# A list schedule made three times: due times of loads that know the kernel's own transposes, a third x buffer and another spacing of score units

## The chip, the cores and the metric

The kernel runs on one core of a Trainium2 chip. The metric is the time of one execution on the device in microseconds (us), less being better; every version is timed over several runs, and one further execution of each is taken with the hardware profiler. The core's engines are TensorE (PE, the matmuls; its weight loads are listed as PEld), VectorE (DVE), ScalarE (ACT), GpSimd (POOL) and SyncE (SP). Each works through its own instructions in program order, and they wait for each other by semaphores. Transfers run on the core's DMA engines; here SP, POOL and once ACT issue them.

## What is computed

Attention over a sliding window of 128 tokens with 4 sink tokens that all may see, 4 batches of 8 heads, 768 tokens, 64 elements a head; then, on the 3072 tokens of 512 elements, a gated feed-forward with two products more. There is no softmax beyond the attention's, so that the last two matrices can be folded into one.

```
scores = q @ k.T / sqrt(64)
keep   = (key < 4) | (0 <= query - key < 128)
x      = softmax(where(keep, scores, -1e9)) @ v        # heads side by side: 3072 x 512
h      = ((x @ w1) * (x @ w2)) @ w3                    # 1024 wide
out    = h @ w_out                                     # 3072 x 512, float32
```

## The kernel before

All matmuls are in bfloat16. w3 and w_out are multiplied once at the start: w3 is transposed on PE (`fold_w3`, L402 to 414) and multiplied with w_out (`fold_mm`, L427), so that each token tile needs one projection. Five of the eight row blocks of w3 and all of w_out come as float32 through SP ("raws", L142, L162) and are cast by ACT and DVE (L418); the other w3 rows, w1, w2, and all of q, k and v come through POOL, which casts on the way (L104 to 139), in the order of the list `order` (L146).

The attention goes batch by batch (b), tile by tile of 256 tokens (t = 0 to 2), head pair by head pair (r = 0 to 3). A unit of scores (`scores`, L255, and `block_scores`, L274, for the first two tiles of batch 0) is: the score matmuls into one of two large PSUM buffers, the exponential on ACT, the mask on DVE. Then `values` (L335, L299) multiplies with v on PE, and DVE divides by the row's sum and writes the result into a buffer xn (L357, L320), one for each tile of 256 tokens. Keys and queries must stand transposed: for batches 0 and 1 PE does it (L211, copied by DVE at L213), a block of 128 tokens at a time; for batches 2 and 3 (`XPOSE`) the DMA does it, issued by SP (`transposes_dma`, L216), two DMAs for each block of 128 tokens. The same holds for x: batches 0 and 1 on PE (L330, L367), batches 2 and 3 by a DMA from SP (`x_transposes_dma`, L375), two for each tile.

The feed-forward of a batch goes over chunks of 384 tokens (256 in batch 0). A gate task (`gate`, L384) makes 128 of the 1024 columns for a chunk: four matmuls with w1, which ACT copies to SBUF, and four with w2, which DVE multiplies with that copy. A first gate of a 384-token chunk reads xT of one tile and a half. A projection (`project`, L448) is eight matmuls for 128 tokens, a copy by ACT and a store by SP.

What stands when on each engine is settled while the program is built. Every piece of work is a task with a priority, a list of stages (engine and cost in us), the tasks it follows, the loads it needs and its kind of PSUM buffer (`task`, L519 and on). The loop from L732 on is a list scheduler: it keeps a clock for each engine, takes for PE the task that can begin soonest and, of those that can begin at once, the one of the lowest priority number, and emits its instructions. A score unit may begin only PACE us after the one before (L660, L698; the index is the tile, or for batch 0's block units their number). The gates and projections have high priority numbers; they fill what is left. When a load is due is worked out beforehand by `landings` (L481): two queues, SP's raw loads and POOL's, each load with a service time, a lag and a share of the DMA engines. SP's queue is one of the scheduler's engines (costs of 1.3 and 1.4 for a transpose, `XP_US` 8.0 and `XX_US` 6.0 until it has landed, L517, L567, L628). POOL's loads are not scheduled; they are emitted in `order`. Where PE would be idle early on, `keep_busy` (L462) puts matmuls on zeros in.

Since the engines work in program order, the schedule sets only the order; the times on the chip follow from it and from what the waits find.

Of the kernel before, what the change touches and what calls it, by code (L numbers as in the profile page):

```python
# [21 lines left out]
def kernel(  # L22
# [276 lines left out]
    def block_values(b, j, r0):  # L299

        t, i = j // 2, j % 2
        av = ps_mm.tile([P, 2, 2, D + 1], FP32, tag="mm", name="av")
        todo = []
        for r in range(r0, r0 + 2):
            if t > 0:
                q0 = (t - 1) * 256 + i * P
                todo.append((av[:, r - r0, :, :].rearrange("p e d -> p (e d)"), es[b][:, q0:q0 + P],
                             vs[b][:, 2 * r:2 * r + 2, :].rearrange("p e d -> p (e d)")))
            am, kbs = ams.pop((b, j, r))
            for s, kb in enumerate(kbs):  # L310
                for e in range(2):
                    todo.append((av[:, r - r0, e, :], am[:, e, s, :], vN[b][:, kb, 2 * r + e, 0:D + 1]))
        for n, (o, lhs, rhs) in enumerate(todo):
            nc.tensor.matmul(o, lhs, rhs, start=(n == 0), stop=(n == len(todo) - 1),  # L314
                             skip_group_check=True)
        yield
        rec = work.tile([P, 2, 2, 1], FP32, tag="rec", name="rec")
        nc.vector.reciprocal(rec[:], av[:, :, :, D:D + 1])
        if i == 0 and r0 == 0:
            xns[b, t] = work.tile([P, 2, NP, 2, D], BF16, tag="xn", bufs=2, name="xn")  # L320
        nc.vector.tensor_mul(xns[b, t][:, i, r0:r0 + 2, :, :], av[:, :, :, 0:D],
                             rec[:].to_broadcast([P, 2, 2, D]))
        yield
# [11 lines left out]
    def values(b, r, t):  # L335
# [20 lines left out]
        if r == 0:  # L356
            xns[b, t] = work.tile([P, 2, NP, 2, D], BF16, tag="xn", bufs=2, name="xn")  # L357
# [123 lines left out]
    def landings(RAW=2.0, POOL=3.0, DGE=1.3, RAMP=(0.33, 0.64, 0.66, 0.9)):  # L481

        queues = {"sp": [(RAW, 1.31, 1.0, [("raw",) + x[:3]]) for x in raws],
                  "pool": [(gen, us, 2.2, keys) for x in order for gen, us, keys in service(*x)]}
# [3 lines left out]
        while any(at[n] < len(q) for n, q in queues.items()):  # L488
            while len(ready) < len(queues["pool"]) and (len(ready) < 8 or len(landed) > len(ready) - 8) \
# [6 lines left out]
                ready.append(max(5.8, issue + DGE))  # L496
            busy = [n for n, q in queues.items() if at[n] < len(q)
# [15 lines left out]
    landings()  # L513

    tasks = {}
    SP_US = 0.7
    XP_US, XX_US = 8.0, 6.0  # L517
# [40 lines left out]
    for b in range(B):  # L558
        for t in range(NT):
# [66 lines left out]
            if b in X_XPOSE:  # L626
                for i in range(2):
                    task(("xd", b, t, i), 1, x_transposes_dma(b, t, i), [("sp", 1.3), ("dma", XX_US)],  # L628
                         [("av", b, NP - 1, t)])
# [30 lines left out]
    PACE = [0.0, 3.4, 3.5, 5.5]  # L660
    TURN, SHAPE = 0.095, {"sc": 1, "ss": 2}
    last_sc, shape = 0.0, 0
    START, WARM_UNTIL = 1.2, 40.0
    BACKLOG = 1.6
    free = {"pe": 0.0, "act": 0.0, "dve": 0.0, "sp": 0.0}
    rings = {n: [[0.0] for _ in range(k)] for n, k in (("mm", 4), ("sc", 2))}
    done, begun = {}, set()
    queue = {"act": [], "dve": [], "sp": []}

    def spare(ring):  # L670
        return sorted((c for c in rings[ring] if c[0] is not None), key=lambda c: c[0])

    def occupy(ring, cell):
        old = spare(ring)[0]
        rings[ring] = [c for c in rings[ring] if c is not old] + [cell]

    def pe_pick():
        best = None
        for k in tasks.values():
            kind = k["name"][0]  # L680
            if k["name"] in begun or any(a not in begun for a in k["started"]) \
                    or k["stages"][0][0] != "pe":
                continue
            if any(a not in (begun if k["half"] else done) for a in k["after"]):
                continue
            est = max([free["pe"]] + [arrive[x] + HOP for x in k["loads"]])
            if not k["half"]:
                est = max([est] + [done[a] + HOP for a in k["after"]])
            if k["ring"]:
                slots = spare(k["ring"])[:k["slots"]]  # L690
                if len(slots) < k["slots"]:
                    continue
                est = max([est] + [c[0] + HOP for c in slots])
            if est > free["pe"]:
                est += MARGIN.get(kind, 0.0)
            if k["paced"]:
                busy = max(0.0, free["act"] - free["pe"]) + sum(q[2] for q in queue["act"])
                est = max(est, free["pe"] + busy - BACKLOG, last_sc + (PACE[k["name"][1]]))  # L698
            wait = est - free["pe"]
            key = (0.0 if wait < 0.05 else wait, k["prio"])  # L700
            if best is None or key < best[0]:
                best = (key, k, est)
        return best

    def when(q):

        at, _, _, k = q
        if k["half"]:
            return max(at, done[k["after"][0]] + HOP) if k["after"][0] in done else None
        return at  # L710

    def advance(k, at):

        i = k["stage"]
        if k["ring"] and i == 1:
            k["cell"][0] = at
        if i == 1 and "frees" in k:
            tasks[k["frees"]]["cell"][0] = at
        k["stage"] = i + 1
        if i + 1 < len(k["stages"]):  # L720
            e, us = k["stages"][i + 1]
            if e == "dma":
                k["stage"] += 1
                done[k["name"]] = at + us
                return
            queue[e].append((at + HOP, YIELD.get(k["name"][0], 0.1), us, k))
        else:
            done[k["name"]] = at

    later = [x for x in order if x[0] == "qkv" and x[1] > 0]  # L730
    folds = [x for x in tasks if x[0] in ("c", "t3", "fm")]
    while len(done) < len(tasks):  # L732
        if later and all(x in done for x in folds):
            for x in later:
                load(*x)
            later = []
        for k in tasks.values():
            e, us = k["stages"][0]
            if e != "pe" and k["name"] not in begun and all(a in done for a in k["after"]):
                begun.add(k["name"])  # L740
                k["stage"] = 0
                at = max([arrive[x] for x in k["loads"]] + [done[a] for a in k["after"]])
                queue[e].append((at + HOP, YIELD.get(k["name"][0], 0.0), us, k))
        pe = pe_pick()
        moves = [(pe[2], 0, "pe")] if pe else []
        picks = {}
        for e in ("act", "dve", "sp"):
            ready = [(max(free[e], when(q)) + q[1], when(q), n)
                     for n, q in enumerate(queue[e]) if when(q) is not None]
            if ready:  # L750
                picks[e] = queue[e][min(ready)[2]]
                moves.append((max(free[e], when(picks[e])), 1, e))
        start, _, e = min(moves)
        if e == "pe":
            k = pe[1]
            gap = start - max(free["pe"], START)
            if gap > 0.5 and start < WARM_UNTIL and spare("mm") \
                    and spare("mm")[0][0] <= max(free["pe"], START):
                keep_busy(int((gap - 0.25) / (0.22 if start > 9.0 else 0.43)))
                occupy("mm", [max(free["pe"], START)])  # L760
            begun.add(k["name"])
            k["stage"] = 0
            us = k["stages"][0][1]
            if SHAPE.get(k["name"][0], 0) != shape:
                shape = SHAPE.get(k["name"][0], 0)
                us += TURN
            if k["paced"]:
                last_sc = start
            if k["ring"]:
                k["cell"] = [None]  # L770
                occupy(k["ring"], k["cell"])
        else:
            q = picks[e]
            queue[e].remove(q)
            us, k = q[2], q[3]
        next(k["gen"])
        free[e] = start + us
        advance(k, free[e])
# [34 lines left out]
```

## Time and profile before

| | |
|---|---|
| median of 3 runs | 198.18 us |
| their range | 197.58 to 199.52 us |
| the profiled execution, its own time | 197.96 us |
| its span, first to last instruction | 196.3 us |
| mean granted clock of TensorE | 0.998 |
| DMA packets, bytes | 104165, 28.35 MB |
| the same, mean over the span | 144 GB/s |

The page gives the busy time of each engine and the chain of work that ended last. The chain in order of time lists its pieces with start, length and name; a piece with x8 is eight instructions of one kind. The timeline lists an engine's instructions, with idle time before them in brackets and what ended it. The DMA view gives packets, bytes and the time from issue to landing; narrowed to one issue, its line is about that one transfer. Lines such as L452 are those of the kernel above. In a row of the windows stand the stretch, the busy time of each engine with its number of instructions, the granted clock, the share of the DMA engines and GB/s.

### The profile page before, as it was taken

What the parts mean: (1) busy time and instruction counts of PE and PEld (TensorE: products, weight loads), DVE (VectorE), ACT (ScalarE), POOL (GpSimd) and SP (SyncE); (2) the same over time, 40 slices, a digit from 0 to 9 for tenths busy, and PEclk for the clock granted to TensorE, in tenths of its full rate; (3) what the DMA queues carried; (4) which work ended last, traced back from release to release, by engine and by line L of the source; (5) the groups of instructions that cost most, each with busy time, mean ns of one, the idle gap of its engine ahead of it and who ended that gap; (6) DMA issues with size and microseconds to landing.
All of it is one profiled execution on the core that took longest, in us unless ns stands there. A gap on an engine that the chain in (4) does not pass through costs nothing.

```text
span 196.3 us, 4494 instructions
## 1 busy us (share of the span) xinstructions
PE 188.9 (96%) x1781; PEld 118.8 (61%) x1795; DVE 114.6 (58%) x268; ACT 105.2 (54%) x174; POOL 75.4 (38%) x104
## 2 busy tenths in 40 slices
PE   7799999999999999999999999999999999999994
PEld 2345566898856687666666655666555566654443
DVE  4455787764876878687879738777644034440000
ACT  4242557845726788886777255556653333332332
POOL 5199878579999853555364300000000000000000
PEclk9999999999999999999999999999999999999999
DMA  6999999999999999999999999930222600002334
GB/s 225 395 365 154 182 163 197 194 158 154 155 155 210 186 172 123 154 168 175 127 130 157 119 155 129 168 79 2 53 110 107 183 33 3 0 0 98 142 141 157
DMA packets 104165, 28.35 MB, mean 144 GB/s; under 512 B 95184, under 2 KB 99664, under 8 KB 104144
## 3 DMA queue, kind: packets, MB, share of 16 engines
q0 software_dynamic: 79520, 12.33, 91.8%
q1 hardware_dynamic: 24480, 15.67, 36.6%
q8 instruction: 14, 0.23, 0.5%
q14 instruction: 7, 0.06, 0.1%
q10 hardware_dynamic: 144, 0.07, 0.1%
HBM read 29.36 MB, written 6.29 MB: 182 GB/s over the span
## 4 chain that ended last, share of the span: by engine, by line
PE 86%; DMA 7%; DVE 3%; issue 1%; ACT 1%; SPq 1%; POOL 0%
PE pg L391 41%; PE po L452 19%; PE av L351 6%; PE sc L261 5%; DMA qN<-in_q_dram 4%; PE pw L438 3%; DMA ab<-in_moe_w_dram 3%; PE ph L438 3%; PE tp L211 2%; PE tp L408 1%; PE av L314 1%; PE xt L367 1%; PE sc L282 1%; DVE w3t L413 1%; PE sp L243 1%
## 5 line engine op out<-in xcount | busy, mean ns | idle before, releaser
L391 PE MATMUL pg<-xT,w_sb 128*128 128x384 bf16 (+1 forms) x576 | 91.0, 308 | 0.0
L391 PEld LDWEIGHTS <-w_sb 128*128 128x128 bf16 x576 | 53.6, 98 | 25.4 <-issue 0.5
L395 DVE TENSOR_TENSOR ab<-a_sb,pg 128x384 bf16<-128x384 f32 (+1 forms) x72 | 36.6, 508 | 29.0 <-PE pg L391 24.9
L398 ACT COPY a_sb<-pg 128x384 f32<-128x384 f32 (+1 forms) x72 | 31.9, 444 | 36.1 <-DVE ab L395 17.7
L452 PE MATMUL po<-w3o,ab 128*128 128x512 bf16 (+2 forms) x198 | 42.6, 362 | 0.5
L266 ACT ACTIVATE ex<-sc 128x1024 bf16<-128x1024 f32 (+1 forms) x40 | 37.8, 964 | 5.4 <-PE sc L261 4.8
L452 PEld LDWEIGHTS <-ab 128*128 128x128 bf16 x208 | 19.3, 98 | 20.1 <-issue 0.3
L456 ACT COPY w_sb<-po 128x512 f32<-128x512 f32 (+2 forms) x25 | 14.1, 565 | 26.0 <-PE po L452 24.1
L270 DVE TENSOR_TENSOR am<-ex,maskt 128x1024 bf16<-128x1024 bf16 (+1 forms) x40 | 25.4, 645 | 3.8 <-ACT ex L266 3.8
L108 POOL DMA_DIRECT2D vN<-in_v_dram x24 | 21.5, 894 | 12.1 <-DMA kN<-in_k_dram 11.2
L108 POOL DMA_DIRECT2D qN<-in_q_dram x24 | 21.7, 904 | 7.9 <-DMA vN<-in_v_dram 5.8
L108 POOL DMA_DIRECT2D kN<-in_k_dram x24 | 21.8, 908 | 7.3 <-DMA qN<-in_q_dram 4.2
L358 DVE TENSOR_TENSOR xn<-av,rec 128x256 bf16<-128x256 f32 x40 | 17.0, 424 | 1.4
L351 PE MATMUL av<-vN,am 128*128 128x65 bf16 x296 | 16.4, 193 | 0.0
L351 PEld LDWEIGHTS <-am 128*128 128x128 bf16 x296 | 14.3, 97 | 2.5 <-issue 0.2
L355 DVE RECIPROCAL rec<-av 128x4 f32<-128x4 f32 x40 | 7.2, 179 | 11.5 <-PE av L351 11.3
L261 PE MATMUL sc<-kqT 64*128 64x128 bf16 (+1 forms) x216 | 11.6, 238 | 0.0
L351 PE MATMUL av<-vs,es 128*128 128x130 bf16 x56 | 11.0, 221 | 0.1
L213 DVE COPY kqT<-tp 128x1024 bf16<-128x1024 bf16 x12 | 8.3, 691 | 4.4 <-PE tp L211 4.3
L438 PE MATMUL ph<-wo_sb,w3t 128*128 128x512 bf16 x32 | 8.6, 380 | 1.4 <-ACT wo_sb L418 0.9
L456 DVE COPY w_sb<-po 128x128 f32<-128x128 f32 x1 | 0.3, 292 | 16.3 <-ACT w_sb L456 16.3
L261 PEld LDWEIGHTS <-kqT 64*128 64x128 bf16 x216 | 6.9, 94 | 4.0 <-issue 3.2
(71 smaller groups left out, 143.9 us busy)
## 6 DMA issues: line engine op xcount, KB each, us to landing
out_dram<-w_sb SPq DMA_DIRECT2D x23, 256.0 KB, 2.2
kN<-in_k_dram POOLq DMA_DIRECT2D x24, 128.0 KB, 8.2
qN<-in_q_dram POOLq DMA_DIRECT2D x24, 128.0 KB, 8.0
vN<-in_v_dram POOLq DMA_DIRECT2D x24, 128.0 KB, 7.8
w_sb<-in_moe_w_dram POOLq DMA_DIRECT2D x9, 256.0 KB, 8.9
ab<-in_moe_w_out_dram SPq DMA_DIRECT2D x3, 512.0 KB, 5.8
ab<-in_moe_w_dram SPq DMA_DIRECT2D x3, 512.0 KB, 6.6
kN<-in_moe_w_out_dram SPq DMA_DIRECT2D x1, 512.0 KB, 8.9
```

What stands on the lines that cost most here:

```text
L108: nc.gpsimd.dma_start(out=dst, in_=rows(src, b, kb))
L261: nc.tensor.matmul(sc[:, e, c:c + n], kT[b][hp, r, kb * P:(kb + 1) * P], qT[b][hp, r, qb * P:qb * P + n], start=True, stop=True)
L266: nc.scalar.activation(ex[:, :, c0:], sc[:, :, c0:], ACTF.Exp, scale=scale)
L270: nc.vector.tensor_mul(am[:, :, c0:], ex[:, :, c0:], mk)
L351: nc.tensor.matmul(o, lhs, rhs, start=(n == 0), stop=(n == len(todo) - 1), skip_group_check=True)
L358: nc.vector.tensor_mul(xns[b, t][:, :, r, :, :], av[:, :, :, 0:D], rec[:].to_broadcast([P, 2, 2, D]))
L391: nc.tensor.matmul(pg[:], w_sb[:, kk, dt * P:(dt + 1) * P], xT[b][:, kk, tk], start=(kk == 0), stop=(kk == NP - 1))
L395: nc.vector.tensor_mul(ab[b][:, dt, tk], gate_a.pop((b, c, dt))[:], pg[:])
L398: nc.scalar.copy(a_sb[:], pg[:])
L438: nc.tensor.matmul(po, w3T[i][:, j, :], wo_sb[:, j, :], start=(j == 0), stop=(j == KFF - 1))
L452: nc.tensor.matmul(po[:], ab[b][:, kk, m * P:(m + 1) * P], w3o[:, kk, n0:n1], start=(kk == 0), stop=(kk == KFF - 1))
L456: (nc.vector.tensor_copy if n0 == DM // 2 else nc.scalar.copy)(o_sb, po[:])
```

## The change

The scheduler becomes a function `plan(emit)`, and it runs three times. The first two runs emit nothing; they return at which times SP would issue its DMAs (`taken`), and the next call of `landings` holds up all loads by 1.2 us for each transpose and by 0.6 us for each store, from 4 us after its issue on. The third run emits the program. Before, the loads of q and k of batches 2 and 3 had a flat 1.2 us more of service time instead.

The constants of `landings` change too (service time, lag and ramp in the diff). A DMA transpose counts as landed 8.4 us after its issue, 5.0 us late in the loads and 2.7 us after the last of them, for 8.0 and 6.0 before. PACE goes from 3.4, 3.5, 5.5 to 4, 4.5, 4.5. The buffers xn are three for two. No computing instruction is added or removed but for the matmuls on zeros, of which four go; the order of the tasks changes on PE, ACT, DVE and SP. POOL's instructions keep their order, and one of its loads (the last block of k of batch 1) waits for PE too.

On SP, the stores and transposes stand in another order. Of the transposes in batches 2 and 3, before had (k, q: blocks of 128 tokens of batch 3; x: tiles of 256 tokens of batch 2)

```
k0  x0 x0  q0 k1 q1  x1 x1  k2 q2 k3 q3  x2 x2  (store)  k4 q4 k5 q5
```

and the changed kernel has

```
k0 q0 k1 q1 k2 q2  x0 x0  k3 q3 k4  x1 x1  q4 k5  (store)  q5  (store)  x2 x2
```

The core of the diff, the indentation of the loop's body left out:

```diff
-            xns[b, t] = work.tile([P, 2, NP, 2, D], BF16, tag="xn", bufs=2, name="xn")
+            xns[b, t] = work.tile([P, 2, NP, 2, D], BF16, tag="xn", bufs=3, name="xn")
...
-            return [(0.95 if i[0] == 0 else 0.87, 0.845 + (1.2 if i[0] in XPOSE and x != "v" else 0.7 if (x, *i) == ("v", 0, 4, 5) else 0.0), [(x, i[0], kb)])
+            return [(0.95 if i[0] == 0 else 0.87, 0.845, [(x, i[0], kb)])
...
-    def landings(RAW=2.0, POOL=3.0, DGE=1.3, RAMP=(0.33, 0.64, 0.66, 0.9)):
+    def landings(taken, RAW=2.0, POOL=3.0, DGE=1.3, RAMP=(0.6, 0.95, 0.85, 0.9)):
-        queues = {"sp": [(RAW, 1.31, 1.0, [("raw",) + x[:3]]) for x in raws],
-                  "pool": [(gen, us, 2.2, keys) for x in order for gen, us, keys in service(*x)]}
+        queues = {"sp": [(RAW, 1.28, 1.0, [("raw",) + x[:3]]) for x in raws],
+                  "pool": [(gen, us, 1.8, keys) for x in order for gen, us, keys in service(*x)]}
+        taken, owed = sorted((t + 4.0, us) for t, us in taken), 0.0
...
+            while taken and taken[0][0] <= now:
+                owed += taken.pop(0)[1]
+            if owed > 0.0:
+                owed -= 0.02
+                now += 0.02
+                continue
...
-    landings()
-    XP_US, XX_US = 8.0, 6.0
...
-                        task(qk[-1], 1, transposes_dma(src, dst, kb), [("sp", 1.4), ("dma", XP_US)],
+                        task(qk[-1], 1, transposes_dma(src, dst, kb), [("sp", 1.4), ("dma", 1.2)],
...
-    PACE = [0.0, 3.4, 3.5, 5.5]
+    PACE = [0.0, 4, 4.5, 4.5]
...
+    def plan(emit):
...
-                done[k["name"]] = at + us
+                    end = max(arrive.values())
+                    done[k["name"]] = at + (8.4 if at < end - 4.0 else 5.0 if at < end else 2.7)
...
+            if e == "sp":
+                taken.append((start, 1.2 if k["name"][0] != "p" else 0.6))
+            if emit:
+                next(k["gen"])
...
+    taken = []
+    for last in (False, False, True):
+        landings(taken)
+        taken = plan(last)
```

More of the change, by code (lines that the diff above doesn't have):

```diff
@@ L356, in values @@
         if r == 0:
-            xns[b, t] = work.tile([P, 2, NP, 2, D], BF16, tag="xn", bufs=2, name="xn")
+            xns[b, t] = work.tile([P, 2, NP, 2, D], BF16, tag="xn", bufs=3, name="xn")
         nc.vector.tensor_mul(xns[b, t][:, :, r, :, :], av[:, :, :, 0:D],
@@ L627 @@
                 for i in range(2):
-                    task(("xd", b, t, i), 1, x_transposes_dma(b, t, i), [("sp", 1.3), ("dma", XX_US)],
+                    task(("xd", b, t, i), 1, x_transposes_dma(b, t, i), [("sp", 1.3), ("dma", 1.2)],
                          [("av", b, NP - 1, t)])
@@ L659 @@
     YIELD = {"g": 0.0, "av": 0.0, "sc": 0.4, "tdk": 1.5, "tdq": 1.5}
-    PACE = [0.0, 3.4, 3.5, 5.5]
+    PACE = [0.0, 4, 4.5, 4.5]
     TURN, SHAPE = 0.095, {"sc": 1, "ss": 2}
-    last_sc, shape = 0.0, 0
     START, WARM_UNTIL = 1.2, 40.0
     BACKLOG = 1.6
[L665 to L691, printed above, removed]
-                    continue
[L693 to L723, printed above, removed]
-                done[k["name"]] = at + us
[L725 to L728, printed above, removed]
@@ L740 @@
                 begun.add(k["name"])
                 k["stage"] = 0
[L742 to L775, printed above, removed]
@@ L776 @@
-        next(k["gen"])
-        free[e] = start + us
-        advance(k, free[e])
+                us = k["stages"][0][1]
+                if SHAPE.get(k["name"][0], 0) != shape:
+                    shape = SHAPE.get(k["name"][0], 0)
+                    us += TURN
+                if k["paced"]:
+                    last_sc = start
+                if k["ring"]:
+                    k["cell"] = [None]
+                    occupy(k["ring"], k["cell"])
+            else:
+                q = picks[e]
+                queue[e].remove(q)
+                us, k = q[2], q[3]
@@ L781 @@
+            if e == "sp":
+                taken.append((start, 1.2 if k["name"][0] != "p" else 0.6))
+            if emit:
+                next(k["gen"])
+            free[e] = start + us
+            advance(k, free[e])
+        return taken
+    taken = []
+    for last in (False, False, True):
+        landings(taken)
+        taken = plan(last)
 _INS = ['q', 'k', 'v', 'n_sink', 'window', 'moe_w1', 'moe_w2', 'moe_w3', 'moe_w_out']
```

97 lines of the change are left out of this document (87 added, 10 removed).

## The prediction

> **What bounds the kernel now.** I read the page first, then the waits, then the chain in order of time.
>
> ```profile
> span 196.3 us, 4494 instructions
> PE 188.9 (96%) x1781; PEld 118.8 (61%) x1795; DVE 114.6 (58%) x268; ACT 105.2 (54%) x174; POOL 75.4 (38%) x104
> PE 86%; DMA 7%; DVE 3%; issue 1%; ACT 1%; SPq 1%; POOL 0%
> ```
>
> TensorE (PE) is busy for 96% of the span. A busy share can hide stretched work, so the waits come next.
>
> ```profile
> PE pz L466 <- DVE ksbd L171: 1.3, 1, 1.3
> PE ph L438 <- ACT wo_sb L418: 0.9, 1, 0.9
> PE pw L438 <- DVE w3t L413: 0.4, 1, 0.4
> PE tp L211 <- DMA qN<-in_q_dram: 0.4, 1, 0.4
> PE ph L438 <- DVE w3t L413: 0.3, 1, 0.3
> ```
>
> 3.3 us in all, 1.3 of it ahead of the first instruction. A new order can win very little and can lose much. What PE's work costs shows in the chain (start, us, what):
>
> ```profile
> 20.20 0.33 PE sc L282 x8
> 22.38 0.45 PE tp L211 x8
> 24.37 0.55 PE sc L282 x16
> 33.56 1.75 PE pg L391 x16
> 60.13 0.44 PE sc L261 x8
> 143.15 1.73 PE po L452 x8
> 149.34 0.71 PE av L351 x20
> 155.23 20.80 PE pg L391 x128
> 187.09 6.26 PE po L452 x44
> ```
>
> Start to start, a gate matmul takes 0.163 us (384 columns) or 0.109 (256), a projection of eight matmuls 1.73, a score matmul 0.028 (eight more cost 0.22). So of the 0.33 us of eight score matmuls 0.11 is the turn to their 64-row shape. PE ends at 187.09 + 6.26 = 193.35. Between the last wait for raw weights (13.74, below) and that end, the pitches times the counts of the program's order fill 177.9 of 179.6 us: gates 62.5 + 20.9, projections 41.6, folds 10.8, av 14.4 (0.36 for ten), scores 9.6, transposes 10.2 (0.056 each), the small rest 1.8, 57 turns 6.0. Only 1.7 us after 13.74 is waiting.
>
> **The change part by part.**
>
> *PE's work.* The changed order holds the same matmuls, but 15 warm-up matmuls for 19, and 59 turns of shape for 57: +0.2 us. The warm-up ones cost nothing, for they fill waits:
>
> ```profile
> 1.33 4.83 PE L466 MATMUL pz<-ksbd 128*128 128x512 bf16 x15 [1.33 <-DVE ksbd L171]
> 8.63 0.59 PE L438 MATMUL ph<-wo_sb,w3t 128*128 128x512 bf16 x2 [0.92 <-ACT wo_sb L418]
> 13.12 2.08 PE L438 MATMUL ph<-wo_sb,w3t 128*128 128x512 bf16 x8 [0.30 <-DVE w3t L413]
> 12.64 1.04 ACT L418 CAST wo_sb<-kN 128x1024 bf16<-128x1024 f32 x1 [1.51 <-DMA kN<-in_moe_w_out_dram]
> ```
>
> The second pair of the row at 13.12 needs the last wo rows, whose cast ACT ends at 12.64 + 1.04: it starts at 13.74. Up to there both orders run through the same raw loads and casts in turn, so that the new due times for these (about 1 us earlier) win nothing. From 13.74 on, the changed order without any wait would end at 193.35 - 1.7 + 0.2 = 191.9. That is the floor, 1.5 us under before.
>
> *Loads of batches 0 and 1.* Before let PE reach each tile late. The changed plan believes in landings about 2 us earlier, and its order goes up to the edge. The last tile is the one that counts: the q half of the last PE transposes.
>
> ```profile
> 62.68 0.39 PE L211 MATMUL tp<-ident,qN 128*128 128x128 bf16 x4
> ```
>
> ```profile
> 55.00 0.92 POOL L108 DMA_DIRECT2D qN<-in_q_dram  x1
> ```
>
> ```profile
> qN<-in_q_dram POOLq DMA_DIRECT2D x1, 128.0 KB, 6.9
> ```
>
> That load (the DMA view narrowed to the one issue) lands at 61.9. Ahead of this point the changed order has one projection less (-1.73), four x transposes more (+0.22) and two turns more (+0.21): 1.30 us less work. Before reached it at 62.68 after 1.6 us of waits, so without waits the changed order is there at 62.68 - 1.62 - 1.30 = 59.76, and it must wait 2.2 us, in small pieces at the loads before it or at once. POOL issues these loads in the same order (its one new wait, on PE at batch 1's last k, is for folded w3 that PE is done with some 25 us before) and the DMA engines are full (155 GB/s, below), so they won't land earlier. The rest is then 193.35 - 62.68 + 1.73 - 0.22 = 132.2, and the end 61.95 + 132.2 = 194.1: +0.8 us. The DVE wait of before (0.4) and this load's neighbour (0.4) fall away; this takes their place.
>
> *SP's queue and batch 3.* SP issues in program order: the DMA transposes of k and q (L218), those of x (L378), the stores.
>
> ```profile
> 93.49 1.19 SPq L218 DMA_TRANSPOSE kqT<-kN  x1
> 94.77 3.91 SPq L378 DMA_TRANSPOSE xT<-xn  x2
> 98.78 2.44 SPq L218 DMA_TRANSPOSE kqT<-qN  x1
> 104.42 3.15 SPq L378 DMA_TRANSPOSE xT<-xn  x2
> 107.67 2.42 SPq L218 DMA_TRANSPOSE kqT<-kN  x1
> 118.87 1.23 SPq L218 DMA_TRANSPOSE kqT<-kN  x1
> ```
>
> Before, the x transposes of batch 2's tiles 0 and 1 go out at 94.77 and 104.42, ahead of k block 2 (107.67) and k block 4 (118.87) of batch 3. The changed queue has tile 0 behind q block 2, and tile 1 behind k block 4, as that k is due at 107.7 by the new plan's own `landings`. The trace has it land here:
>
> ```profile
> 100.81 0.88 POOL L108 DMA_DIRECT2D kN<-in_k_dram  x1
> ```
>
> ```profile
> kN<-in_k_dram POOLq DMA_DIRECT2D x1, 128.0 KB, 15.4
> ```
>
> At 116.2, 8.5 us later. Everything behind that k transpose on SP waits with it: tile 1's x transposes, then q block 4, block 5, two stores, tile 2. Who waits for tile 1 is PE, in its own order: the first gate of batch 2 reads tokens 0 to 383, so both transposes of tile 0 and the first of tile 1.
>
> ```profile
> 114.76 1.48 PE L391 MATMUL pg<-xT,w_sb 128*128 128x384 bf16 x8
> ```
>
> That is this gate in before. The changed order has three projections (5.20), two av of 6 matmuls (0.37), two score units (0.33) and four turns (0.42) more ahead of it: 6.3 us. It is reached at 114.76 - 1.67 + 6.3 + 2.2 = 121.6. The transpose lands so:
>
> ```profile
> 40.00:58.00 18.00, 17.95 (x202) 14.13 (x202) 11.79 (x25) 9.76 (x19) 16.56 (x20) 1.00 2.49 155
> 93.00:121.00 28.00, 27.95 (x287) 17.35 (x285) 20.71 (x49) 16.62 (x28) 8.81 (x11) 1.00 1.91 141
> ```
>
> ```profile
> q0 software_dynamic: 15646, 1.97, 128.6%
> q1 hardware_dynamic: 7929, 1.92, 61.9%
> ```
>
> ```profile
> 80.94 0.87 POOL L108 DMA_DIRECT2D kN<-in_k_dram  x1 [0.68 <-DMA vN<-in_v_dram]
> ```
>
> ```profile
> kN<-in_k_dram POOLq DMA_DIRECT2D x1, 128.0 KB, 12.4
> xT<-xn SPq DMA_TRANSPOSE x1, 8.7
> ```
>
> (The two queue rows are of the DMA view from 93 to 121: packets, MB, share. The last rows: the first k of batch 3 lands at 80.94 + 12.4 = 93.3; an x transpose takes 8.7 us from issue at 115.19, the busy time.) The last two numbers of the windows are the DMA engines' share and GB/s: they move 155 GB/s with loads alone and 141 with transposes among them, so both cost by their bytes. From 93.3 to 116.2 twelve loads and eleven transposes landed, 23 blocks of 128 KB, 0.99 us each. In the changed order the four x transposes are behind, and one more q transpose is ahead: about eight instead of eleven, so k block 4 lands at 93.3 + 20 x 0.99 = 113.2. Its own issue takes 1.25, and the x transpose 8.7: 123.2. Bounds: not before PE asks (121.6, no wait), and at most 116.2 + 1.25 + 8.7 = 126.2, if the loads are no faster. I take 123.2, since the count is what changed; PE waits 1.6 us. After it 193.35 - 114.76 - 5.9 - 0.2 = 72.5 us of work remain, which take the end to 195.7. Later transposes (tile 2, blocks 4 and 5) are asked for 15 us later and have time.
>
> *The rest.* The third x buffer adds no instruction; it frees DVE from the wait for x transposes 8.7 us under way, a wait that PE's list does not show: no gain; if DVE did wait for tile 0 it would land near 117, ahead of the write at about 119. The spacing of score units (4, 4.5, 4.5 for 3.4, 3.5, 5.5) puts batch 2's later and batch 3's earlier; ACT and DVE, at 54% and 58%, cover it. Cost 0, between -0.4 (the DVE wait of before, gone or not) and +0.6 (a kqT copy that DVE has behind its w3t copies near 28 us), and the load at 61.9 takes up either.
>
> *Sum.* 195.7 for 193.35: +2.4 us on the profiled execution's 197.96, so 200.3. The median of the runs is 198.18, 0.2 above it; I don't add that.
>
> **The rivals.**
>
> *A: tile 1 in time.* A load of 128 KB is some 1,024 packets (1.97 MB in 15,646) and 0.85 us at 155 GB/s, a transpose some 512 (1.92 MB in 7,929). If it cost the loads only that share, 0.43 us, k block 4 would land at 93.3 + 12 x 0.85 + 8 x 0.43 = 106.9, about where the plan has it, the x transpose near 117, and only the first wait is left: 194.1, so 198.7 us, not slower by what can be told. It decides from k landing before 111.6 on. Against it: 23 blocks took 22.9 us. The Trainium skill, "DMA: Bandwidth & Descriptors", section on queues, rings and completion order, has each engine alternate between queues packet by packet, which would give rival A's price if all packets cost alike; by that rule the sum is 198.7. The trace does not bear that out: 141 GB/s against 155 says that a transpose's packets, twice as large, cost twice.
>
> *B: faster.* If the loads of batch 1 landed 2.2 us earlier (and A holds), the floor of 191.9 is reached: 196.5 us, 1.5 under the profiled execution. It breaks even at 0.8 us earlier. For it: the plan's landing times for batch 1 are 1 us earlier than the trace's from its fourth block on. Against it: full DMA engines and POOL's unchanged order.
>
> *C: the loads are no faster.* The transposes that leave are made up by others that move up: 126.2, end 198.7, 203.3 us. For it: SP's queue refills with whatever is ready. Against it: q block 2 and later can't go before their loads.
>
> **How the numbers follow.** Forecast 0.5, A 0.25, B 0.05, C 0.2. The likeliest gives 200.3. Low 198.5 takes in A and leaves out B; high 203.2 nearly takes in C. A measurement of this kernel can tell about 1% (2 us). A and B lie within 1% (B beyond it for a part, 0.03); the forecast's own range, 199.2 to 201.8 by 1.2 us either way in the landing, crosses +1% at 200.2: 0.32 of its 0.5 lies beyond, 0.52 with C. So faster 0.03, same 0.45, slower 0.52.
>
> **What would show it.** Right: PE waits at L211 for kN, qN or vN of batches 0 and 1, about 2 us in all between 40 and 62; then one wait ahead of pg L391 at about 121.6, released by xT<-xn, 1 to 5 us; no other after it; the end of PE 2.4 us later. Wrong: no wait before that gate (A), PE through its last transposes before 61 (B), or waits at sc L261 for kqT in batch 3, which I have in time by 7 us and more.

## The result and the profile after

Over 22 runs each, the changed kernel takes 199.37 us (median; 197.43 to 200.22) and the kernel before 198.18 us (196.82 to 200.16). The ratio is 1.0058, with a 95% interval of 1.004 to 1.0075: 0.6% slower, 1.2 us. The profiled execution took 198.79 us; that of before took 197.96.

The page of the changed kernel: the span, the engines, and the shares of the chain that ended last.

```profile
span 197.1 us, 4495 instructions
...
PE 189.2 (96%) x1777; PEld 118.6 (60%) x1791; DVE 115.2 (58%) x268; ACT 105.6 (54%) x174; POOL 75.7 (38%) x104
...
PE 69%; DMA 20%; POOL 6%; issue 2%; SPq 1%; ACT 0%; DVE 0%; POOLq 0%
```

PE is as busy as before, to the per cent. What has changed is the chain: loads held 7% of it and now hold 20%, and POOL, which issues them, 6%. The waits of PE (total us, times, longest):

```profile
PE pz L466 <- DVE ksbd L171: 1.3, 1, 1.3
PE ph L438 <- ACT wo_sb L418: 0.8, 1, 0.8
PE ph L438 <- DVE w3t L413: 0.6, 2, 0.3
PE tp L211 <- DMA qN<-in_q_dram: 0.6, 2, 0.4
PE tp L408 <- DVE w_sb L418: 0.3, 1, 0.3
PE tp L211 <- DVE w3t L413: 0.2, 1, 0.2
```

The chain in order of time (start, length), between 40 and 62 us and at its end:

```profile
41.99 7.05 DMA vN<-in_v_dram
49.04 0.05 issue
49.09 0.39 PE vp L232
...
52.51 6.84 DMA qN<-in_q_dram
59.35 0.05 issue
59.40 0.40 PE tp L211 x4
...
187.92 6.26 PE po L452 x44
```

PE ends at 187.92 + 6.26 = 194.18, 0.8 us later than before (193.35). The loads stand in the chain where the prediction had its first wait: PE is through its transposes only as fast as q and v land. The last load that holds it is the q of block 4 of batch 1 (59.35). Against its own pitches (the time from one start to the next where nothing waits, as in the prediction), the order has lost 2.05 us by there since the raw weights came in at 13.68. The list's waits at L211 are only a part of this; the rest shows as starts later than the pitches allow (0.27 us at 49.09, where v has landed at 49.04, and 0.14 to 0.37 us at a few other places). Not all of it is for loads of q, k and v: the list has 0.2 us at L211 behind DVE's copy of w3.

At the second place, SP's transposes, the gate of batch 2, and two single transfers (the DMA view narrowed to the issues at 98.29 and 114.43):

```profile
98.29 0.88 POOL L108 DMA_DIRECT2D kN<-in_k_dram  x1 [0.50 <-DMA qN<-in_q_dram]
...
113.11 1.23 SPq L218 DMA_TRANSPOSE kqT<-kN  x1
114.43 2.53 SPq L378 DMA_TRANSPOSE xT<-xn  x2
```

```profile
kN<-in_k_dram POOLq DMA_DIRECT2D x1, 128.0 KB, 14.8
...
xT<-xn SPq DMA_TRANSPOSE x1, 7.1
```

```profile
121.05 0.50 PE L261 MATMUL sc<-kqT 64*128 64x256 bf16 x8
121.69 0.81 PE L391 MATMUL pg<-xT,w_sb 128*128 128x384 bf16 x4
```

k block 4 of batch 3 landed at 98.29 + 14.8 = 113.1, its transpose went out at 113.11, and tile 1's first x transpose at 114.43. That one landed at 121.55, and the gate begins at 121.69. The list has no wait here, but the starts do. In the kernel "batch 3 later", below, PE's order is the same and tile 1 had landed at 116.5; there the gate begins 0.44 us after the first of these eight score matmuls:

```profile
119.89 0.50 PE L261 MATMUL sc<-kqT 64*128 64x256 bf16 x8
120.33 0.82 PE L391 MATMUL pg<-xT,w_sb 128*128 128x384 bf16 x4
```

Here PE could have begun the gate at 121.05 + 0.44 = 121.49. It began 0.2 us later, 0.14 us after the transpose had landed, as in three of the four executions below in which the list has this wait. (The chain names ACT's copy of the projection before it, which ended at 121.56; but with batch 3 later the gate begins while that copy still runs, at 120.33 for 120.40.) So PE was held by the transpose here too, for 0.2 us. The expectations below were worked out with a margin of 0.1 us in its place.

### The profile page after: what moved, and what is told of

Same layout as the page of the kernel before. It is cut to its first block, busy times and chain, and to the rows that moved or that the text cites. A ratio compares the mean times of both kernels' runs of the same rounds, so it can differ in the third digit from the quotient of the medians.

```text
span 197.1 us, 4495 instructions
## 1 busy us (share of the span) xinstructions
PE 189.2 (96%) x1777; PEld 118.6 (60%) x1791; DVE 115.2 (58%) x268; ACT 105.6 (54%) x174; POOL 75.7 (38%) x104
## 4 chain that ended last, share of the span: by engine, by line
PE 69%; DMA 20%; POOL 6%; issue 2%; SPq 1%; ACT 0%; DVE 0%; POOLq 0%
PE pg L391 37%; PE po L452 20%; DMA w_sb<-in_moe_w_dram 9%; PE av L351 6%; PE sc L261 5%; DMA ab<-in_moe_w_out_dram 4%; DMA vN<-in_v_dram 4%; DMA qN<-in_q_dram 3%; POOL w_sb L111 2%; POOL qN L108 1%; POOL kN L108 1%; POOL vN L108 1%; PE xt L367 1%; SPq L162 1%; PE tp L211 1%
## 5 line engine op out<-in xcount | busy, mean ns | idle before, releaser
L391 PE MATMUL pg<-xT,w_sb 128*128 128x384 bf16 (+1 forms) x576 | 92.0, 308 | 0.1
L286 ACT ACTIVATE ex<-sc 128x1024 bf16<-128x1024 f32 x7 | 7.0, 1026 | 5.6 <-PE sc L282 5.6
L438 PE MATMUL ph<-wo_sb,w3t 128*128 128x512 bf16 x31 | 8.0, 380 | 1.6 <-ACT wo_sb L418 0.8
```

The source lines that it names most:

```text
L391: nc.tensor.matmul(pg[:], w_sb[:, kk, dt * P:(dt + 1) * P], xT[b][:, kk, tk], start=(kk == 0), stop=(kk == NP - 1))
```

## The experiments

Theory: the loss is PE waiting for loads of batches 0 and 1, because the new due times put the order at the landings; and tile 1 of x, behind k block 4 on SP, stands so close to PE's first gate of batch 2 that it costs there, in some runs at least. Rivals: the spacing or the buffer costs the time; the two added turns of shape do (0.2 us); the four matmuls on zeros that went do, through the clock.

For every profiled execution the table gives when PE passed the last raw weights (the second pair of the fold matmuls of one row at L438, 13.74 in before), its end, the difference, and the timed result. The first column varies from 13.0 to 15.6 us, though the loads and casts ahead of it are the same in all. (The 15.60 has a second cause: in that execution the granted clock was 0.5 from 10.9 to 14.3 us.) This start is a part of the spread of each kernel's runs, some 3 us from lowest to highest; so the ratios are compared by their intervals, and the difference column shows where a profile differs. The ratios are those on record; the quotient of two medians differs from them by up to 0.2% (0.9997 for "both later", 1.0045 for "changed, again").

| kernel | raw weights | PE's end | difference | median us | ratio to before, 95% |
|---|---|---|---|---|---|
| before | 13.74 | 193.3 | 179.6 | 198.18 | 1 |
| changed | 13.68 | 194.2 | 180.5 | 199.37 | 1.0058 (1.004 to 1.0075) |
| changed, again | 14.20 | 194.0 | 179.8 | 198.82 | 1.0059 (1.0031 to 1.0086) |
| spacing and buffer alone | 14.23 | 193.4 | 179.2 | 198.22 | 1.0002 (0.998 to 1.0023) |
| old spacing, 3 buffers | 13.27 | 193.7 | 180.4 | 198.95 | 1.0044 (1.0012 to 1.0076) |
| old spacing, 2 buffers | 15.60 | 202.7 | 187.1 | 207.35 | 1.0469 (1.0425 to 1.0512) |
| changed, 2 buffers | 13.71 | 197.9 | 184.2 | 203.44 | 1.0282 (1.0236 to 1.0328) |
| batch 1 later | 14.81 | 195.7 | 180.9 | 199.34 | 1.006 (1.0035 to 1.0084) |
| batch 3 later | 13.08 | 192.8 | 179.7 | 198.88 | 1.003 (1.0003 to 1.0056) |
| both later | 13.16 | 192.3 | 179.1 | 197.86 | 1.0015 (0.9987 to 1.0042) |
| due as seen | 13.96 | 192.9 | 179.0 | 197.80 | 0.9996 (0.9968 to 1.0024) |
| tile 1 behind q block 4 | 14.15 | 195.5 | 181.4 | 199.94 | 1.0078 (1.0049 to 1.0107) |
| one plan | 13.02 | 201.4 | 188.4 | 205.13 | 1.0349 (1.0298 to 1.0399) |

The runs of before beside these had medians of 197.87 to 198.12 us. By the changed order's own pitches the difference would be 178.1 without any wait.

The clock of TensorE does not make the loss. Of the 22 runs of the changed kernel four have a mean granted clock of 0.991, which is the size of one stretch of 3.4 us at 0.5. But the twelve runs of its repetition have none below 0.998 and the same ratio.

**The spacing and the buffer alone**, on the kernel before:

```diff
-    ... tag="xn", bufs=2, ...
+    ... tag="xn", bufs=3, ...
-    PACE = [0.0, 3.4, 3.5, 5.5]
+    PACE = [0.0, 4, 4.5, 4.5]
```

> The kernel before with only the third x buffer and the new spacing of score units (4, 4.5, 4.5); its due times and its single plan stay. My theory (the loss of the change is PE waiting for loads of batches 0 and 1, because the new due times put the order at or ahead of the landings): no loss here. By the order and the landings of the profiled runs PE waits 1.9 us for loads, as in before, and ends at 193.45 against 193.35; 198.0 to 198.5 us, ratio to before 0.998 to 1.003. Rival S (the spacing or the buffer costs the time): the whole loss of the change is here, ratio 1.005 or more.

Measured 198.22 us, 1.0002: in the order of before, neither costs nor wins anything. The chain of its page is PE's again:

```profile
PE 92%; DMA 4%; DVE 2%; SPq 1%; issue 1%; ACT 0%
```

The rival that blames the spacing or the buffer falls; the due times remain, alone or together with them.

**Batch 1's loads due later**, in the changed kernel:

```diff
-                        arrive[key] = now + lag
+                        arrive[key] = now + lag + (1.3 if key[0] in "kqv" and key[1] == 1 else 0.0)
```

> The changed kernel with the due times of batch 1's loads 1.3 us later in its planner, nothing else. My theory: the waits for loads between 47 and 60 us go (1.2 us of 2.3), and PE then reaches the first gate of batch 2 at 120.4 instead of 121.7. The x transposes of tile 1 stay behind k block 4 on SP and landed at 121.55 in the changed kernel's profile, so of the 1.2 us some 1.1 come back as a wait at that gate, released by xT: end of PE 194.0, time 198.5 to 199.4 us, ratio to before 1.002 to 1.006. Rival L (loads are the whole of it, tile 1 lands early enough): end of PE 192.8, 197.5 us, ratio 0.995 to 0.998. Rival S (spacing): no change against the changed kernel, and no wait at the gate.

Measured 199.34 us, 1.006: nothing won. Its profile has no wait for loads between 47 and 60 any more, but one at 45 for q block 4 of batch 0, which this edit left at the edge (it landed late in this execution, in which the raw weights were late too), and the wait at the gate:

```profile
45.46 0.40 PE L211 MATMUL tp<-ident,qN 128*128 128x128 bf16 x4 [1.21 <-DMA qN<-in_q_dram]
123.22 0.81 PE L391 MATMUL pg<-xT,w_sb 128*128 128x384 bf16 x4 [0.26 <-DMA xT<-xn]
```

The direction is the theory's, and the gate's wait is where it was expected, but at 0.3 us it isn't the 1.1 us that would have taken the whole gain back: PE was there some 2.5 us later than I had put it. So this run by itself doesn't show where the gain went.

**Batch 3's loads due later**: 6.0 for `key[1] == 3` in the same place. PE's order is unchanged; on SP, tile 1's x transposes go ahead of k block 4.

> The changed kernel with batch 3's loads due 6 us later in its planner: PE's order stays the same to the last instruction, and on SP the x transposes of tiles 0 and 1 move ahead of k blocks 2 and 4. If some runs of the changed kernel hold a wait at the first gate of batch 2 that its profiled run misses by 0.1 us, the median falls, by 0.3 to 0.6 us: 198.8 to 199.1, ratio to before 1.002 to 1.004. If no run has that wait: 199.3, ratio 1.005 to 1.007, the same as the changed kernel. In both cases x tile 1 lands well before 121 us, PE waits about 2.1 us for loads before 60, and the end of PE in the profile stays at 194.1.

Measured 198.88 us, 1.003 against 1.0058: what the case with a gate wait in some runs expected. The intervals overlap, so by itself it isn't decided.

**The changed kernel again**, without an edit:

> The changed kernel once more, as it is, beside the others of this call on one chip: 199.4 us, ratio to before 1.004 to 1.0075. In its profile PE waits about 2.1 us for loads of batches 0 and 1 and for w3 rows between the anchor near 13.7 and 60 us; whether it waits at the first gate of batch 2 goes by where tile 1's x transpose lands (121.55 in the first profile, 0.1 us ahead of PE).

Measured 1.0059. Its profile has the wait at the gate:

```profile
121.51 0.81 PE L391 MATMUL pg<-xT,w_sb 128*128 128x384 bf16 x4 [0.34 <-DMA xT<-xn]
```

The first of the score matmuls ahead of it began at 120.66, so that the gate starts 0.4 us late, 0.3 us of it idle. The first profile lost 0.2 us here.

This execution shows two things more. The raw weights came in 0.5 us later than in the first, but PE was at q block 4 of batch 1 at 59.01 instead of 59.40: it had waited less on the way. The difference column is 179.8 for 180.5. So two executions of one program differ there by 0.7 us, and no single profile can divide the loss. And k block 4 of batch 3 landed at 110.7 (issued at 98.02, 12.7 us), 2.4 us earlier than in the first. SP came to its transpose only at 112.88, since the one before it held SP for 2.66 us:

```profile
110.13 2.66 SPq L218 DMA_TRANSPOSE kqT<-qN  x1
112.88 1.28 SPq L218 DMA_TRANSPOSE kqT<-kN  x1
```

Tile 1's x transposes went out at 114.26, for 114.43 in the first.

**Tile 1 behind one transpose more**: `-5.0 if key in (("k", 3, 4), ("q", 3, 4)) else 0.0` in the same place. PE's order is unchanged; SP has q block 4 ahead of tile 1 too.

> The changed kernel with k and q of batch 3's block 4 due 5 us earlier in its planner: PE's order stays the same to the last instruction, and on SP the x transposes of tile 1 stand behind one transpose more, that of q block 4, which landed at 114.63. They go out at about 116.0 and take 6.4 to 7.1 us: PE, which asks for them at 121.7, waits 0.7 to 1.4 us ahead of that gate, released by xT; end of PE 194.9 to 195.6, 199.5 to 200.3 us, ratio to before 1.008 to 1.014. Were this place covered, nothing would change: 199.3, ratio 1.005 to 1.007.

Measured 199.94 us, 1.0078. SP and PE in its profile, and tile 1's first transfer:

```profile
118.67 3.20 SPq L378 DMA_TRANSPOSE xT<-xn  x2
...
123.03 0.81 PE L391 MATMUL pg<-xT,w_sb 128*128 128x384 bf16 x4 [1.11 <-DMA xT<-xn]
```

```profile
xT<-xn SPq DMA_TRANSPOSE x1, 4.2
```

The wait is there, 1.1 us. The transposes went out later than expected (118.67, not 116.0) and took 4.2 us instead of 6.4 to 7.1, when the loads had nearly all landed (the last at 118.86). This bears on the prediction's mis-sized term, below.

**Both later**: 1.3 for batch 1 and 6.0 for batch 3.

> The changed kernel with batch 1's loads due 1.3 us later and batch 3's 6 us later in its planner: PE's order is that of the run with batch 1 later alone, but the x transposes of tiles 0 and 1 go out ahead of k blocks 2 and 4. My theory (two places, and the second takes back what the first gives unless both are moved): the 1.2 us are won now, end of PE 192.8, 197.1 to 198.0 us, ratio to before 0.995 to 0.999. Rival G (tile 1 is no limit, the run with batch 1 later was slow for another reason): no change against that run, ratio 1.004 to 1.008.

Measured 197.86 us, 1.0015 (0.9987 to 1.0042); the ratio's middle lies above what my theory expected and below rival G's. Its profile has no wait for q, k, v or xT in the list; by the middles, of the changed kernel's 0.6%, 0.4% are won (1.0058 to 1.0015), no more. The two intervals overlap a little (the one begins at 1.004, the other ends at 1.0042).

**Due as seen**: k, q and v due at their landings in the changed kernel's trace, plus 0.9 us for batches 0 and 1 and 2.0 us for batches 2 and 3.

```diff
-                        arrive[key] = now + lag
+                        arrive[key] = SEEN.get(key, now + lag)
```

> The changed kernel with the due times of all k, q and v loads taken from the landings in its own profile, 0.9 us later for batches 0 and 1 and 2 us later for batches 2 and 3. By its order and those landings PE waits 0.4 us for loads of batches 0 and 1, its x tiles go out early on SP (gate of batch 2 asked for at 118.4, tile 1 behind q block 2 of batch 3... landing near 117). My theory: end of PE 192.1 to 192.5, 196.6 to 197.4 us, ratio to before 0.992 to 0.997, faster than both kernels. Rival N (the order is at the floor already and what is won at the loads comes back elsewhere, at copies on DVE or at the start): ratio 0.998 to 1.004.

Measured 197.80 us, 0.9996. The interval lies below that of the changed kernel, whose loss is gone altogether, with the same spacing, buffers and three plans. By its trace it has the same 59 turns of shape and the same 15 matmuls on zeros, too, so that neither of these makes the loss. But it is rival N's time against before, not mine. PE's waits in it:

```profile
PE ph L438 <- ACT wo_sb L418: 1.1, 1, 1.1
PE tp L408 <- DVE w_sb L418: 0.9, 2, 0.5
PE ph L438 <- DVE w3t L413: 0.3, 1, 0.3
```

None of them is for a load of q, k or v. A reason that fits, and that I have only argued: where PE waits for loads, a late start is taken up by those waits, so removing them wins only in runs that start early. The kernel with the spacing alone passed the raw weights 0.5 us later than before did and ended level with it (193.4); due as seen passed them 0.2 us later and ended 0.4 us earlier, and 0.4 us is 0.2%, within its interval.

**The due times alone**, the changed kernel with the old spacing and two buffers:

> The changed kernel with the old spacing (3.4, 3.5, 5.5) and two x buffers: the due times and the three plans alone. By its order and the landings of the changed kernel's profile PE waits 1.7 us for loads before 60 (before: 1.9), has 0.3 us more turns of shape, and reaches the first gate of batch 2 at 118.0; its x tile 1 goes out behind k block 3 of batch 3, not k block 4, and lands near 117, so no wait at the gate. My theory (loads at the edge, and tile 1 behind k block 4): end of PE 193.6, 198.0 to 198.6 us, ratio to before 0.999 to 1.003. Rival D (the new due times cost their time with any spacing): ratio 1.004 to 1.0075, as the changed kernel.

Measured 207.35 us, 1.0469: both theories fall. SP, DVE and PE in its profile:

```profile
99.87 3.75 SPq L378 DMA_TRANSPOSE xT<-xn  x2
```

```profile
110.71 0.42 DVE L358 TENSOR_TENSOR xn<-av,rec 128x256 bf16<-128x256 f32 x1 [6.55 <-DMA xT<-xn]
```

```profile
111.19 0.29 PE L351 MATMUL av<-vs,es 128*128 128x130 bf16 x1 [5.30 <-DVE xn L358]
```

SP issues tile 0's second transpose at 101.14 (the second of the row's two), and it lands 9.4 us later. DVE's write of tile 2's x goes into the buffer from which tile 0 is still being transposed. DVE stands for 6.55 us with everything that is queued behind it, and PE for 5.30. Then the clock (stretch, PE, PEld, DVE, ACT, POOL busy, granted clock, DMA share, GB/s):

```profile
105.00:106.00 1.00, 0.89 (x6) 0.31 (x4) 0.00 (x0) 1.00 (x3) 0.87 (x1) 1.00 1.63 156
109.00:110.00 1.00, 0.00 (x0) 0.00 (x0) 0.00 (x0) 0.00 (x0) 0.00 (x0) 0.95 2.36 153
113.00:114.00 1.00, 1.00 (x5) 0.50 (x4) 0.29 (x2) 0.00 (x0) 0.00 (x0) 0.50 1.64 155
116.00:117.00 1.00, 1.00 (x6) 0.47 (x4) 0.53 (x1) 0.00 (x0) 0.00 (x0) 0.63 1.66 153
117.00:118.00 1.00, 1.00 (x16) 0.73 (x15) 0.33 (x3) 0.48 (x1) 0.00 (x0) 1.00 1.84 154
```

PE idles from 105.9; from about 109.9 its granted clock is 0.5, and full again only at about 116.7. Two kernels were to tell the buffers from the spacing.

**Two x buffers** in the changed kernel, all orders the same:

> The changed kernel with two x buffers instead of three: the orders of PE, DVE, ACT and SP stay the same to the last instruction. With two, DVE's first write of tile 2's x (at 112.0 in the changed kernel's profile) must wait for tile 0's transposes, which landed there at 115.4: 3.4 us on DVE, and the first write of batch 3 (119.5) for tile 1's, 122.1, where some of the first wait has moved it already. In the run of the due times alone a wait of 6.5 us on DVE was 5.3 us on PE, so 1.2 us are slack here: PE waits about 2.1 us at av, and the 0.3 us at the gate go. End of PE 195.9, 200.3 to 201.5 us, ratio to before 1.012 to 1.020; if PE's clock drops behind that wait as it did behind the 5.3 us, up to 3 us more. Rival (the third buffer is worth nothing, as in the order of before): 1.004 to 1.0075.

Measured 203.44 us, 1.0282: above the 1.012 to 1.020 expected without the clock, and within the 3 us more that were named for it:

```profile
115.33 0.42 DVE L358 TENSOR_TENSOR xn<-av,rec 128x256 bf16<-128x256 f32 x1 [3.61 <-DMA xT<-xn]
```

```profile
116.41 0.40 PE L351 MATMUL av<-vN,am 128*128 128x65 bf16 x4 [2.65 <-DVE am L270]
```

```profile
113.00:114.00 1.00, 0.76 (x5) 0.20 (x2) 0.00 (x0) 0.94 (x2) 0.00 (x0) 1.00 1.61 158
115.00:116.00 1.00, 0.00 (x0) 0.00 (x0) 0.67 (x2) 0.00 (x0) 0.00 (x0) 0.97 1.68 153
116.00:117.00 1.00, 0.59 (x10) 0.60 (x10) 0.95 (x2) 0.00 (x0) 0.00 (x0) 0.50 1.67 164
119.00:120.00 1.00, 1.00 (x6) 0.34 (x4) 0.07 (x1) 0.00 (x0) 0.00 (x0) 0.83 1.47 104
```

DVE waits 3.6 us (expected 3.4), PE 2.7, and the clock falls behind that too. In this order the third buffer carries 1.0282 - 1.0058 = 2.2%, about 4.4 us.

**The old spacing with three buffers**, `PACE` alone put back:

> The changed kernel with the old spacing (3.4, 3.5, 5.5) alone; the third x buffer stays. Theory B (the 9 us of the run with old spacing and two buffers come from the buffers alone): no wait at av for xn; tile 1 of batch 2 goes out behind k block 3 and lands near 117, ahead of the gate at 118.0; PE waits 1.7 us for loads; end of PE 193.6, 198.0 to 198.6 us, ratio to before 0.999 to 1.004. Rival S (it is the spacing with the new due times): 203 us or more, with the wait at av still there.

Measured 198.95 us, 1.0044, above theory B's 0.999 to 1.004 by a hair: no wait at av for xn, so rival S falls, and the third buffer alone makes the difference between 207.35 and 198.95 us. Its middle is nearer to the changed kernel's ratio than to 1. In its profile PE waits for loads as in the changed kernel, and the gate, reached at 117.97, is free. So, by the middles, most of the loss is there without the gate; the interval, from 1.0012 on, leaves room.

**One plan** instead of three, `for last in (True,)`:

> The changed kernel with the schedule made once instead of three times: the landings are then worked out without the planner's own transposes and stores. PE's order is the same up to about 116 us. Batch 3's loads are believed earlier still, and on SP all six k and six q transposes of batch 3 but one stand ahead of tile 1's x transposes. k block 5 landed at 118.4 in the changed kernel's profile, its q block a microsecond later: tile 1 goes out at about 121 and lands at 124.5 to 126, while PE, in this order, asks for it at 117.3. PE waits 7 to 9 us ahead of the gate, and its clock may drop behind that as it did behind the wait of 5.3 us (3 us more): end of PE 201 to 206, 205 to 211 us, ratio to before 1.035 to 1.065. Rival (SP's order in batch 3 has cover of a few us): no more than 2 us over the changed kernel, 1.016 or less.

Measured 205.13 us, 1.0349, just under the lower end expected:

```profile
119.56 2.52 SPq L378 DMA_TRANSPOSE xT<-xn  x2
```

```profile
122.08 4.02 PE L391 MATMUL pg<-xT,w_sb 128*128 128x384 bf16 x12 [6.03 <-DMA xT<-xn]
```

```profile
xT<-xn SPq DMA_TRANSPOSE x1, 2.5
```

Tile 1 goes out at 119.56, 1.4 us ahead of what I had worked out, and lands 2.5 us later; the last load had landed at 120.0. PE waits 6.0 us, and its clock falls:

```profile
120.00:121.00 1.00, 0.00 (x0) 0.00 (x0) 0.00 (x0) 0.00 (x0) 0.00 (x0) 0.67 1.09 191
126.00:127.00 1.00, 1.00 (x10) 0.66 (x9) 0.49 (x2) 0.48 (x1) 0.00 (x0) 0.50 0.93 240
127.00:128.00 1.00, 1.00 (x8) 0.51 (x6) 0.49 (x2) 0.00 (x0) 0.00 (x0) 0.91 0.30 61
```

So the plans that know of the transposes are worth some 2.9% (1.0349 - 1.0058), given the other new constants.

## Why the prediction came out as it did

*PE's work.* Right: nothing moved but the turns, and the order with the fewest waits (due as seen) needs 179.0 us behind the raw weights, where the prediction's floor was 178.2 (191.9 - 13.7).

*Loads of batches 0 and 1.* Right in kind, and in size for the first profile: 2.2 us of waits were predicted, 2.05 us of lost time found, and PE's end with this wait alone was to be 194.1 and is 194.2, 0.2 us at the gate included. Some of the agreement is luck: a part of the 2.05 is spent at copies of w3, and the second execution lost 0.9 us less by the same point (59.01 - 14.20 = 44.81 for 59.40 - 13.68 = 45.72). The place was off within its bounds: the waits are spread over the loads up to q block 4 of batch 1, and the last load, 61.9 in before, landed at 61.3 and held nobody. With due times taken from the landings seen, the whole loss goes.

*SP's queue and batch 3.* In the first profile three numbers of the sum were right: k block 4 lands at 113.1 (113.2 predicted, by 20 blocks of 0.99 us), tile 1 goes out at 114.43 (114.45), PE asks at 121.5 (121.6). **The term that was mis-sized is the time of the x transpose: 8.7 us predicted, 7.1 measured**, and with it the wait, 1.6 us predicted and 0.2 in the first profile, 0.4 in the second. The 8.7 was read from a transpose of before at 115.19, with loads on both sides of it. In the changed order the same arithmetic that moved k block 4 forward moves the end of the loads too: the last landed at 121.9, against 127.1 in before. With few loads left, transposes took less. The row for it stood in before's trace, in the same view (the issue at 122.74, with 4.4 us of loads to go):

```profile
kqT<-kN SPq DMA_TRANSPOSE x1, 5.5
```

That the 1.6 us come from the end of the loads fits all these rows, but no run isolates it. In the midst of the loads, too, the transposes of before took from 6.7 us (the issue at 78.80) to 9.6 us (96.12), so that one row could not give the term to better than 1 us or so. With the loads ending, rival C could not happen as priced either: the later tile 1 goes out, the shorter it takes (7.1 us at 114.4, 4.2 at 118.7, 2.5 at 119.6, in kernels whose last loads landed at 121.9, 118.9 and 120.0).

The measured 199.37 lies within the stated range, but between the forecast and rival A. The outcome of the profile is that of rival A (198.7 predicted, 198.8 in the profiled execution), but not its mechanism: A wanted k block 4 before 111.6, by cheap transposes. In the first profile it landed at 113.1. In the second it did land ahead of that, at 110.7, and the gate waited all the same, since SP was still held by the transpose before. Neither the forecast nor A had a price for that: they give each issue 1.25 us, and here one took 2.66 (the prediction's own rows have 2.44 at 98.78). So it is partly luck that tile 1 went out within 0.2 us of the forecast in both. The pricing of transposes by bytes stood: from the first k of batch 3 to its block 4, 20 blocks took 0.99 us each in the first profile, 19 took 0.94 in the second.

*The rest, costed at nothing.* The spacing is right (1.0002). The third buffer's cost of nothing is right in the sum, but the reason given, that it wins nothing because PE's list shows no such wait, holds for the order of before alone. In the new order, x tile 0 goes out behind q block 2, and the third buffer covers a DVE wait of 3.6 us and, behind it, PE's clock. I had named no cover for this edit, and it was the one with the largest price. The prediction's fallback was off as well: it had tile 0 landing near 117, ahead of a write at about 119; in the kernel with two buffers DVE was at that write at 111.7, and tile 0 landed at 115.2.

*Rival B*, faster, failed as priced: the loads of batch 1 landed no more than 0.6 us earlier than the trace of before said (the last q at 61.3 for 61.9), where break-even needed 0.8.

Left open: how the 0.6% divides between the two places. Moving tile 1 alone gives 1.003, moving batch 1 alone 1.006, both 1.0015, and neighbouring intervals overlap. What is shown is that with due times behind the landings there is no loss, and that neither the spacing nor the buffer makes it. That PE's waits are how the due times cost the time is the reading of the traces; the timed runs show the due times as the cause. That a version without these waits doesn't beat the kernel before beyond its interval has the argued reason above, not a shown one.

## What to carry to other kernels

A due time that is exact leaves PE to pay for every load that comes a little late. Here due times with 0.9 us of margin for batches 0 and 1, and 2 us behind them, took the ratio from 1.0058 to 0.9996. When a change moves one transfer of a queue forward, carry the shift through to the end of the traffic before taking a latency from the old trace. And where an edit only adds a buffer, ask what the new order does with one buffer fewer; the old order can't tell.

## What the runs showed of the hardware

A wait of PE can cost more than its length. Behind 2.65 us (two buffers) the granted clock was 0.5 for 3.4 us, from 115.94 to 119.34 by the means of the rows shown. Behind 5.3 us it was 0.5 from 109.9 to 116.7, behind 6.0 us from 120.3 to 127.2: 6.8 us each time, twice 3.4. On top of the waits this cost 1.3 to 2.9 us (what the order lost further against its pitches behind them).

The length of one wait doesn't decide it. The clock stayed at 1.0 behind 1.1 us at the gate (tile 1 behind q block 4) and behind 1.8 us at the folds (batch 1 later, 9.68). But in the profile of the due times alone it was 0.5 from 10.9 to 14.3 us, 3.4 us again, and the longest wait ahead of that was 1.24 us (8.96), with three shorter ones near it (0.53 at 6.19, 0.30 at 7.11, 0.36 at 9.91).

The Trainium skill, "TensorE: Matmul & The Clock Gate", Part 1, The HAM clock gate, has the rate halve after at least one idle window of about 3.4 us that runs freely. The lengths of the four stretches agree with such a window. The 2.65 us don't agree with an idle window in full: the clock fell 2.2 us after PE's last matmul (113.76), so that of the 3.4 us up to the drop the first 1.2 us were matmuls; and in the 3.4 us ahead of the drop at 10.9 us PE had matmuls for about half of the time. There the measurement decides: a wait of 2.65 us can be enough, and so can several short ones.

A DMA transpose of 128 x 512 elements within SBUF took 6.7 to 10.1 us from its issue in the midst of POOL's loads, over all the traces. Behind the last load most took 2.4 to 2.5 us and some, beside another transpose or stores, up to 4.6. The issue itself held SP for 1.2 us at least, and for up to 2.9 us while other transposes were on their way.
